# Polysketch attention with a wave MLP: the numerators of two batches as 32 products of 288 columns on 32x32 tiles

## The chip, the cores and the metric

The kernel runs on one core of a Trainium2 chip. The metric is the device time of one execution in microseconds (us); lower is better. The numbers of the trace come from one profiled execution.

## The reference

Sizes: 4 batches (B), 4 heads (H), 1088 positions (S), head width 32 (D), so 128 channels (DM); the sketch has r = 8.

```python
def phi(x):
    a = np.einsum('rd,bhsd->bhsr', S1, x)
    b = np.einsum('rd,bhsd->bhsr', S2, x)
    return np.einsum('bhsi,bhsj->bhsij', a, b).reshape(*x.shape[:-1], r * r)
q_p, k_p = phi(q), phi(k)
kv = np.einsum('bhsf,bhsd->bhfd', k_p, v)
z = np.sum(k_p, axis=2)
num = np.einsum('bhsf,bhfd->bhsd', q_p, kv)
den = np.einsum('bhsf,bhf->bhs', q_p, z)[..., None] + 1e-06
x = (num / den).transpose(0, 2, 1, 3).reshape(B, S, H * D)

theta = x @ w_theta
y = einsum('ts,bsd->btd', w_tok_r, x * cos(theta)) + einsum('ts,bsd->btd', w_tok_i, x * sin(theta))
u = x + y
out = u + np.maximum(u @ w_ch, 0.0)
```

Everything is f32. The denominators can be small, so the sums ahead of the division are held more exactly than one f32 product would; that is why queries, keys and their sketches are split into parts.

## The kernel before, in words

**Layout.** Positions are cut into NC = 9 chunks of 128 (the last one has 64 positions; the buffers are 9 x 128 = 1152 wide), the chunks into NG = 3 groups of GC = 3, so a group has GW = 384 columns. A fully summed f32 product on PE appears in the trace as two records, one for each part of the f32 operands.

**How the work is ordered.** No loop emits instructions directly. Each function calls `op(engine, estimated duration, closure, written, read)` of the class `Layout` (L203; `vop` is the same for DVE), which numbers the operation. Two tables at the top of the file decide the rest: `ORDER` (L34) lists the operations' numbers in the order in which their instructions are issued, which fixes the order on each engine, and `STARTS` (L80) has a planned start for each. `run` (L248) walks through ORDER and gives each buffer, from the planned starts and ends, one slot of its class (`big`: 22 tiles of 1152 words a partition, `zs` 5 of 2176, `hf` 6, `g3` 5 of 768, `g1` 6 of 384, `sm` 13, `ps`: the 8 PSUM banks of 512). `issue` (L267) emits the operations; in a planned gap on PE in the early part it puts idle products (`spin`, L427). Who waits for whom follows from slots and order: a buffer that takes a slot waits for the last reader of the slot's former buffer.

**Stages.** (1) Loads, and the sums over the keys of each batch: `key_sums`, `kfeatures`, `chain`, `chain_out` give for each batch `kvb[b]`, the sums of key features times values. (2) The w_tok matrices are loaded and prepared as `rows[i]`, 17 tiles of 1088 columns. (3) For each batch `query_slices` transposes and scales the queries; `levels` (L1033) multiplies them by the sketch matrices: for each group of three chunks `exact` issues f16 products of parts, and `whole` (L1050) three f32 products whose stationary operand is a chunk of 128 columns of `f` and whose moving operand is `mf[b]` (96 columns). Then DVE combines the parts, forms the denominators and divides one of the two sketches by them.

(4) `outputs_x` (L1088) forms the numerators. For each group of a batch, DVE multiplies the two sketches of the queries to 64 features for each head and position (`outer` into `qp`). In batches 0 and 1 TensorE transposes these and multiplies them by `kvb`. In batches 2 and 3 (`QUADS`) DVE transposes within squares of 32 (L1109, into `qt`, a `g3` buffer), and `quads` (L1112) issues 32 products on 32x32 tiles of the array: two feature halves f, four position squares j, four heads h; the four squares go to four PSUM banks `xq[j]`, the four heads to four strips of 32 partitions, and the second half adds to the first. Each has 96 moving columns (3 chunks x 32 positions). Four copies on ACT (L1121) put the banks into `xt`, x transposed (channels x positions).

(5) For batches 1 to 3 (`XTURN`, L1149) x is brought back to positions x channels on the way through DRAM: DVE transposes in squares of 32 (L1160), SP stores the tile to `far` (L1161) and fetches it with four DMAs (L1165). For batch 3 x is first scaled on ACT (L1155) by a ratio of the largest values of batches 2 and 3, which `balance` (L1229) finds with DVE reductions over both. Beside it run the products with w_theta, sine and cosine on ACT, and then DVE forms `z` = (x cos, x sin) in a `zs` buffer.

(6) The product with w_tok: for batches 0 and 1 `mix_row` (L1256) sums 17 products a column part. Batches 2 and 3 together go through `winograd` (L1352): seven products of halves instead of eight, of sums of quarters of w_tok (DVE and POOL) and differences of z. Products 1 and 2 need z of batch 2 alone; product 5 (L1429) is the first that needs z of batch 3, in a difference with batch 2 (L1427), so the whole round trip of batch 3 lies ahead of it. (7) `finish` (L1282) adds relu(u @ w_ch), transposes and stores; `finish_turned` (L1329) does this for one piece of batch 3 with TensorE transposes, an ACT copy and two products recorded as one operation, into columns of `xT[3]`.

Of the kernel before, what the change touches and what calls it, by code (L numbers as in the profile page):

```python
# [10 lines left out]
F32 = mybir.dt.float32  # L11
# [67 lines left out]
)  # L79
STARTS = (  # L80
# [58 lines left out]
)  # L139
WARM = 0  # L140
FILL = 5.0
LOAD_LEAD = 60.0
RAW_LEAD = 30.0
CHAINS = ((0,), (1,), (2, 3))
# [35 lines left out]
class Layout:  # L180
# [67 lines left out]
    def run(self):  # L248
        slots = {c: [[0.0, None] for _ in range(n)] for c, (n, _) in self.classes.items()}
        for b in self.bufs:  # L250
            b.left = len(b.ops)
# [52 lines left out]
def act(n):  # L304
    return 0.17 + 0.00083 * n
# [1238 lines left out]
```

## Time and profile before

| what | value |
|---|---|
| three runs | 218.03, 218.3, 219.25 us; median 218.3 |
| span of the profiled execution | 215.9 us |
| median of the runs less that span | 2.4 us |
| granted TensorE clock from 78 us on | 1.00 |
| busy: PE, DVE, ACT, POOL | 208.9, 174.3, 114.5, 59.7 us |
| read from and written to HBM | 29.84 and 4.00 MB |

The page of the profile gives the span of the execution's instructions, not a time of the program, so the span is the profiled execution's own time here; the runs of the table above are timed from outside it. Busy times say how full an engine is; which engine sets the end at a given moment is told by the chain of work that ended last, and by the waits. A timeline row has its start in us, its length in us, engine, line, operation, output<-input, tile shape for PE, operand shape and the number of instructions; rows of PE overlap, since a record lasts until its result is written, so the time that a row costs PE is read from its start to the start of the next.

### The profile page before, as it was taken

What the parts mean: (1) busy time and instruction counts of PE and PEld (TensorE: products, weight loads), DVE (VectorE), ACT (ScalarE), POOL (GpSimd) and SP (SyncE); (2) the same over time, 40 slices, a digit from 0 to 9 for tenths busy, and PEclk for the clock granted to TensorE, in tenths of its full rate; (3) what the DMA queues carried; (4) which work ended last, traced back from release to release, by engine and by line L of the source; (5) the groups of instructions that cost most, each with busy time, mean ns of one, the idle gap of its engine ahead of it and who ended that gap; (6) DMA issues with size and microseconds to landing.
All of it is one profiled execution on the core that took longest, in us unless ns stands there. A gap on an engine that the chain in (4) does not pass through costs nothing.

```text
span 215.9 us, 5832 instructions
## 1 busy us (share of the span) xinstructions
PE 208.9 (97%) x2396; PEld 152.8 (71%) x2396; DVE 174.3 (81%) x343; ACT 114.5 (53%) x256; POOL 59.7 (28%) x105
## 2 busy tenths in 40 slices
PE   7899999999999999999999999999999999999992
PEld 7677798868866666866668666667677776666781
DVE  1799998999999998999999798885994747456263
ACT  4899989999998895798704233363810000000000
POOL 1272740306400000604004100000006489950403
PEclk9999999999999999999999999999999999999998
DMA  6999999995998993192002402424050420010735
GB/s 222 395 418 419 384 365 420 425 315 97 360 285 267 416 432 145 75 308 45 0 0 32 74 3 112 114 109 112 2 88 15 67 39 0 0 23 8 125 55 103
DMA packets 28046, 37.09 MB, mean 172 GB/s; under 512 B 20564, under 2 KB 23044, under 8 KB 25844
## 3 DMA queue, kind: packets, MB, share of 16 engines
q1 hardware_dynamic: 22868, 31.86, 42.4%
q0 software_dynamic: 1552, 3.25, 7.2%
q10 hardware_dynamic: 3600, 1.62, 2.8%
q8 instruction: 19, 0.31, 0.6%
q14 instruction: 7, 0.06, 0.1%
HBM read 29.84 MB, written 4.00 MB: 157 GB/s over the span
## 4 chain that ended last, share of the span: by engine, by line
PE 63%; DMA 18%; ACT 14%; issue 2%; SPq 1%; DVE 1%; POOL 1%; POOLq 0%; ACTq 0%
PE ps L399 61%; DMA zs<-w_tok 13%; DMA big<-k_l 5%; ACT big L645 4%; ACT big L643 3%; ACT lv L1056 1%; PE ps L1131 1%; ACT big L1021 1%; ACT g L1199 1%; ACT g L1202 1%; ACT g L1205 1%; ACT g L1203 1%; POOL out L1299 1%; SPq L671 0%; ACT g L1135 0%
## 5 line engine op out<-in xcount | busy, mean ns | idle before, releaser
L399 PE MATMUL ps<-big,zs 128*128 128x384 f32 (+2 forms) x380 | 110.5, 436 | 0.0
L399 PEld LDWEIGHTS ps<-big,zs 128*128 128x128 f32 x380 | 66.9, 190 | 32.5
L379 POOL TENSOR_TENSOR big<-big,big 128x544 f32<-128x544 f32 x16 | 22.1, 1458 | 48.6 <-DVE big L379 44.6
L399 PE MATMUL ps<-big,big 128*32 128x32 f32 (+2 forms) x352 | 22.8, 234 | 0.0
L643 ACT ACTIVATE big<-zs 128x1088 f32<-128x1088 f32 x17 | 20.9, 1231 | 1.5 <-DMA zs<-w_tok 0.9
L379 DVE CUSTOM_DVE_ANT_0 big<-big,big 128x2176 uint16<-128x2176 uint16 x17 | 21.5, 1275 | 0.0
L645 ACT ACTIVATE big<-zs 128x1088 int32<-128x1088 uint32 (+1 forms) x18 | 21.4, 1194 | 0.3 <-DMA zs<-w_tok 0.3
L1338 ACT COPY big<-ps 80x256 f32<-80x256 f32 x1 | 0.4, 368 | 39.6 <-DMA out<-g 39.6
L399 PEld LDWEIGHTS ps<-big,big 128*32 128x32 f32 (+1 forms) x352 | 15.3, 124 | 6.8 <-issue 0.8
L1276 ACT COPY g<-ps 128x384 f32<-128x384 f32 (+1 forms) x6 | 2.5, 466 | 23.4 <-PE ps L399 23.4
L379 DVE TENSOR_TENSOR big<-big 128x544 f32<-128x544 f32 x8 | 9.5, 1204 | 5.6 <-PE ps L399 5.6
L383 DVE TENSOR_SCALAR big<-big 128x1088 int32<-128x1088 int32 x17 | 12.2, 719 | 0.0
L379 POOL TENSOR_TENSOR mf<-mv,sm 128x32 f32<-128x32 f16 (+1 forms) x3 | 0.8, 262 | 39.1 <-DVE sm L379 39.1
L428 PE MATMUL ps<-idle 128*128 128x112 bf16 (+1 forms) x67 | 10.0, 312 | 1.3 <-POOL idle L430 1.3
L379 DVE TENSOR_TENSOR g<-lv 128x768 f32<-128x768 f32 x12 | 11.1, 950 | 0.1
L399 PEld LDWEIGHTS ps<-w,big 128*128 128x128 f32 (+1 forms) x76 | 9.8, 189 | 1.4
L379 DVE TENSOR_TENSOR big<-big,hf 128x1152 f32<-128x1152 f32 x8 | 10.7, 1351 | 0.0
L399 PE MATMUL ps<-w,big 128*128 128x128 f32 (+1 forms) x76 | 10.5, 278 | 0.0
L399 PE MATMUL ps<-sbk,g 128*128 128x64 f32 x72 | 10.0, 276 | 0.3 <-ACT g L793 0.3
L379 DVE TENSOR_TENSOR zs<-zs,g 128x384 f32<-128x384 f32 (+2 forms) x24 | 9.8, 447 | 0.2
L386 DVE SCALAR_TENSOR_TENSOR big<-ps,even,big 128x384 f32<-128x384 f32 (+1 forms) x10 | 4.8, 493 | 6.3 <-PE ps L399 6.2
L1199 ACT ACTIVATE g<-ps 128x384 f32<-128x384 f32 x12 | 5.9, 504 | 7.3 <-PE ps L399 7.3
(199 smaller groups left out, 379.2 us busy)
## 6 DMA issues: line engine op xcount, KB each, us to landing
zs<-w_tok SPq DMA_DIRECT2D x17, 1088.0 KB, 10.6
big<-k_l SPq DMA_DIRECT2D x5, 576.0 KB, 13.2
big<-v_l SPq DMA_DIRECT2D x4, 576.0 KB, 15.6
big<-q_l SPq DMA_DIRECT2D x3, 576.0 KB, 10.7
big<-hf POOLq DMA_DIRECT2D x3, 576.0 KB, 10.0
far<-zs SPq DMA_DIRECT2D x3, 576.0 KB, 2.8
zs<-far SPq DMA_DIRECT2D x12, 144.0 KB, 4.3
big<-k_l ACTq DMA_DIRECT2D x2, 576.0 KB, 4.4
```

What stands on the lines that cost most here:

```text
L379: eng.tensor_tensor(out=o, in0=a, in1=b, op=f)
L383: (eng or V).tensor_scalar(out=o, in0=a, scalar1=s1, scalar2=s2, op0=op0, **kw)
L386: (eng or V).scalar_tensor_tensor(out=o, in0=a, scalar=s, in1=b, op0=op0, op1=op1)
L399: T.matmul(o, lhs, rhs, start=start, stop=stop, skip_group_check=True)
L428: T.matmul(nowhere()[:, :n], idle()[:, 0:P], idle()[:, :n], start=True, stop=True, skip_group_check=True)
L643: op("A", 0.22 + n * 0.0009, lambda: A.activation(dfn(), words_of(raw(), n)[1].bitcast(F32), AF.Prelu, scale=2.0**-112, alpha=-(2.0**32)), ...
L645: op("A", 0.22 + n * 0.0009, lambda: A.activation(stp(), words_of(raw(), n)[0].bitcast(U32), AF.Copy, scale=2.0**-29), [stp], [raw])
L1021: op("A", act(GW) + 0.1, lambda g=g, tr=tr: A.activation(f()[:, g * GW:(g + 1) * GW], tr(), AF.Copy, scale=s()[:, 0:1]), [(f, g)], [tr, (s ...
L1056: op("A", act(480), lambda g=g, lp=lp: A.copy(lv().rearrange("p l (c n) -> p l c n", n=HR)[:, :, g * GC:(g + 1) * GC], lp().rearrange("p c ...
L1131: T.transpose(tr()[:, i * P:(i + 1) * P], qp()[:, i * H + 2 * n:i * H + 2 * n + 2].rearrange("p h i j -> p (h i j)"), ident())
L1199: op("A", act(GW), lambda cs=cs, th=th: A.activation(cs()[:, 0], th(), AF.Copy, bias=ROUND), [(cs, 0)], [th])
L1276: op("A", act(w), lambda: A.copy(u(), yp()[:, :w]), [uT], [yp])
```

## The change

The numerators of batches 2 and 3. The three DVE transposes of a batch write one common buffer `qt` of the class `zs`, and one block per batch issues 32 products of 288 moving columns (9 chunks x 32 positions), where three groups of 32 products of 96 columns stood. Four PSUM banks per batch hold 288 columns each, and four ACT copies of 288 columns replace twelve of 96. The estimate QUAD goes from 0.65 to 1.25. For the common buffer the class `zs` becomes 2304 words wide; `hf` and `sm` have one slot less.

`whole` in `levels` takes for the last chunk only its 64 positions as stationary columns. `finish_turned` has its own buffer `yb` of the class `g1`, and its transposes, copy and products are three operations; an operation without instructions is gone.

The tables. STARTS and the planning in `run` are gone; `SLOTS` names the slot of each buffer and `GAPS` the number of idle products ahead of an operation. The numbers of ORDER after the numerators are other operations than before, since operations were added and removed; the issue order of the early part is kept, and the part from the numerators on is a new order.

```diff
--- before.py
+++ after.py
 ORDER = (
-    29, 32, 4, 2, 5, 0, 1, 3, 34, ...
+    0, 1, 29, 32, 4, 2, 5, 3, 34, ...
...
-STARTS = (
-    73, 73, 90, 92, 103, 130, ...
+GAPS = {11: 3, 57: 3, 79: 3, 110: 1, 203: 8, 153: 1, 77: 5, 86: 2, 163: 1}
+SLOTS = (
+    0, 5, 1, 3, 5, 0, 3, 9, ...
...
-FILL = 5.0
...
-TILE16, TILE32, TILE64, QUAD = 0.045, 0.12, 0.15, 0.65
+TILE16, TILE32, TILE64, QUAD = 0.045, 0.12, 0.15, 1.25
...
     def run(self):
-        slots = {c: [[0.0, None] for _ in range(n)] for c, (n, _) in self.classes.items()}
...
         self.order = [self.ops[i] for i in ORDER]
-        for o, at in zip(self.order, STARTS):
...
-    def issue(self, pools, fill, span):
-
-        last, on = 0.0, False
+        for b, slot in zip([b for b in self.bufs if b.cls is not None], SLOTS):
+            b.slot = slot
+
+    def issue(self, pools, fill):
         for o in self.order:
-            if o.eng == "P":
-                if on:
-                    for _ in range(int((o.start - last - 0.08) * FILL)):
-                        fill()
-                last, on = o.end, on and o is not span[1] or o is span[0]
+            for _ in range(GAPS.get(o.i, 0)):
+                fill()
...
-        "zs": (5, 2176),
+        "zs": (5, 2304),
...
-        "hf": (6, 576),
+        "hf": (5, 576),
...
-        "sm": (13, 192),
+        "sm": (12, 192),
...
             def whole(g=g, o=o):
                 for i in range(GC):
-                    x = f()[:, (g * GC + i) * P:(g * GC + i + 1) * P]
-                    mm(o(i)[:, 2 * HR:], x, mf[b]().rearrange("p t h r -> p (t h r)"), False, i == GC - 1)
+                    c = g * GC + i
+                    n = min(P, S - c * P)
+                    x = f()[:, c * P:c * P + n]
+                    mm(o(i)[:n, 2 * HR:], x, mf[b]().rearrange("p t h r -> p (t h r)"), False, i == GC - 1)
...
         bd = kvb[b]
+        qt = buf("zs", (NC, H, 2, SQ), F32, "qt") if b in QUADS else None
...
             if b in QUADS:
-                qt = buf("g3", (GC, H, 2, SQ), F32, "qt")
-                xq = [buf("ps", (GC, SQ), F32, "xq") for _ in range(NQ)]
-                vop(CH * R * R, lambda qt=qt, qp=qp: V.transpose(out=qt().rearrange("p c h f t -> p (c h f t)"),
-                                                                 in_=qp().rearrange("p n i j -> p (n i j)")), [qt], [qp])
-
-                def quads(qt=qt, xq=xq):
...
-                op("P", QUAD, quads, xq, [bd, qt], hold=[xt])
-                for j in range(NQ):
-                    op("A", act(GC * SQ), lambda g=g, j=j, xq=xq: A.copy(
-                        xt().rearrange("p (c j t) -> p c j t", j=NQ, t=SQ)[:, g * GC:(g + 1) * GC, j], xq[j]()),
-                       cells(xt, g * GW, (g + 1) * GW), [xq[j]])
+                vop(CH * R * R, lambda g=g, qp=qp: V.transpose(
+                    out=qt()[:, g * GC:(g + 1) * GC].rearrange("p c h f t -> p (c h f t)"),
+                    in_=qp().rearrange("p n i j -> p (n i j)")), [(qt, g)], [qp])
                 continue
...
+        if b in QUADS:
+            at("num", b)
+            xq = [buf("ps", (NC, SQ), F32, "xq") for _ in range(NQ)]
+
+            def quads():
+                for f in range(2):
+                    for j in range(NQ):
+                        for h in range(H):
+                            u = slice(j * SQ, (j + 1) * SQ)
+                            mm(xq[j]()[h * D:(h + 1) * D], bd()[u, f, h], qt()[u, :, h, f], f == 0, f == 1)
+
+            op("P", QUAD, quads, xq, [bd, qt], hold=[xt])
+            for j in range(NQ):
+                op("A", act(NC * SQ), lambda j=j: A.copy(
+                    xt().rearrange("p (c j t) -> p c j t", j=NQ, t=SQ)[:, :, j], xq[j]()), [(xt, ("q", j)) if j < NQ - 1 else xt], [xq[j]])
...
     def finish_turned(b, t0, w, u, keys, due):
         po, pu = (buf("ps", (GW,), F32, x) for x in ("po", "pu"))
         n = w // 2
-        y = lambda: xT[b]()[:n, 0:2 * DM]
+        yb = buf("g1", (2 * DM,), F32, "yb")
+        y = lambda: yb()[:n]
+
+        def turned():
+            for c in range(2):
+                T.transpose(pu()[:n, c * DM:(c + 1) * DM], u()[:, c * n:(c + 1) * n], ident())
 
         def products():
-            parts = [u()[:, c * n:(c + 1) * n] for c in range(2)]
-            for c, uc in enumerate(parts):
-                T.transpose(pu()[:n, c * DM:(c + 1) * DM], uc, ident())
-            A.copy(y(), pu()[:n, 0:2 * DM])
-            for c, uc in enumerate(parts):
-                mm(po()[:n, c * DM:(c + 1) * DM], uc, w2()[:, 1], True, True)
-
-        op("P", w * 4 / 2400 + 0.01, products, [po, pu], keys + [w2])
-        vop(w, lambda: stt(y(), po()[:n, 0:2 * DM], 0.0, y(), ALU.max, ALU.add), keys, [po])
-        vop(w, lambda: None, [], keys)
+            for c in range(2):
+                mm(po()[:n, c * DM:(c + 1) * DM], u()[:, c * n:(c + 1) * n], w2()[:, 1], True, True)
+
+        op("P", 0.2, turned, [pu], keys, hold=[yb])
+        op("A", act(2 * DM), lambda: A.copy(y(), pu()[:n, 0:2 * DM]), [yb], [pu])
+        op("P", 0.35, products, [po], keys + [w2])
+        vop(2 * DM, lambda: stt(y(), po()[:n, 0:2 * DM], 0.0, y(), ALU.max, ALU.add), [yb], [po])
```

More of the change, by code (lines that the diff above doesn't have):

```diff
@@ L248, in run @@
     def run(self):
-        slots = {c: [[0.0, None] for _ in range(n)] for c, (n, _) in self.classes.items()}
-        for b in self.bufs:
-            b.left = len(b.ops)
         self.order = [self.ops[i] for i in ORDER]
-        for o, at in zip(self.order, STARTS):
-            o.start = at / 100.0
-            o.end = o.start + o.dur + o.fly
-            for b in o.bufs:
-                if b.slot is None and b.cls is not None:
-                    free = [(s[0], i) for i, s in enumerate(slots[b.cls]) if s[1] is None]
-                    b.slot = min(free)[1]
-                    slots[b.cls][b.slot][1] = b
-            for b in o.bufs:
-                b.left -= 1
-                b.end = max(b.end, o.end)
-                if not b.left and b.slot is not None:
-                    slots[b.cls][b.slot] = [b.end, None]
-    def issue(self, pools, fill, span):
-        last, on = 0.0, False
-        for o in self.order:
-            if o.eng == "P":
-                if on:
-                    for _ in range(int((o.start - last - 0.08) * FILL)):
-                        fill()
-                last, on = o.end, on and o is not span[1] or o is span[0]
+        for b, slot in zip([b for b in self.bufs if b.cls is not None], SLOTS):
+            b.slot = slot
+    def issue(self, pools, fill):
+        for o in self.order:
+            for _ in range(GAPS.get(o.i, 0)):
+                fill()
             for b in o.bufs:
@@ L430 @@
     op("G", 0.3, lambda: G.memset(idle(), 0.0), [idle], [], due=-20.0)
-    first = op("P", 3.2, lambda: [spin(112) for _ in range(39)], [nowhere], [idle], due=-10.0)
+    op("P", 3.2, lambda: [spin(112) for _ in range(39)], [nowhere], [idle], due=-10.0)
     op("V", 1.25, constants, [hm, bdm, halfpi, ones], [])
@@ L1106, in outputs_x @@
             if b in QUADS:
-                qt = buf("g3", (GC, H, 2, SQ), F32, "qt")
-                xq = [buf("ps", (GC, SQ), F32, "xq") for _ in range(NQ)]
-                vop(CH * R * R, lambda qt=qt, qp=qp: V.transpose(out=qt().rearrange("p c h f t -> p (c h f t)"),
-                                                                 in_=qp().rearrange("p n i j -> p (n i j)")), [qt], [qp])
-                def quads(qt=qt, xq=xq):
-                    for f in range(2):
-                        for j in range(NQ):
-                            for h in range(H):
-                                u = slice(j * SQ, (j + 1) * SQ)
-                                mm(xq[j]()[h * D:(h + 1) * D], bd()[u, f, h], qt()[u, :, h, f], f == 0, f == 1)
-                op("P", QUAD, quads, xq, [bd, qt], hold=[xt])
-                for j in range(NQ):
-                    op("A", act(GC * SQ), lambda g=g, j=j, xq=xq: A.copy(
-                        xt().rearrange("p (c j t) -> p c j t", j=NQ, t=SQ)[:, g * GC:(g + 1) * GC, j], xq[j]()),
-                       cells(xt, g * GW, (g + 1) * GW), [xq[j]])
+                vop(CH * R * R, lambda g=g, qp=qp: V.transpose(
+                    out=qt()[:, g * GC:(g + 1) * GC].rearrange("p c h f t -> p (c h f t)"),
+                    in_=qp().rearrange("p n i j -> p (n i j)")), [(qt, g)], [qp])
                 continue
@@ L1331, in finish_turned @@
         n = w // 2
-        y = lambda: xT[b]()[:n, 0:2 * DM]
-        def products():
-            parts = [u()[:, c * n:(c + 1) * n] for c in range(2)]
-            for c, uc in enumerate(parts):
-                T.transpose(pu()[:n, c * DM:(c + 1) * DM], uc, ident())
-            A.copy(y(), pu()[:n, 0:2 * DM])
-            for c, uc in enumerate(parts):
-                mm(po()[:n, c * DM:(c + 1) * DM], uc, w2()[:, 1], True, True)
-        op("P", w * 4 / 2400 + 0.01, products, [po, pu], keys + [w2])
-        vop(w, lambda: stt(y(), po()[:n, 0:2 * DM], 0.0, y(), ALU.max, ALU.add), keys, [po])
-        vop(w, lambda: None, [], keys)
+        yb = buf("g1", (2 * DM,), F32, "yb")
[3 more added lines that the diff above has]
+                T.transpose(pu()[:n, c * DM:(c + 1) * DM], u()[:, c * n:(c + 1) * n], ident())
+        def products():
+            for c in range(2):
[4 more added lines that the diff above has]
+        vop(2 * DM, lambda: stt(y(), po()[:n, 0:2 * DM], 0.0, y(), ALU.max, ALU.add), [yb], [po])
         def store(E, c):
             E.dma_start(out[b, t0 + c * n:t0 + (c + 1) * n, :], y()[:, c * DM:(c + 1) * DM])
-        op("S", w * P * 2 / 100e3, lambda: store(SY, 0), [], keys, due, lk=2)
-        op("A", 0.92, lambda: store(A, 1), [], keys, due, fly=2.1)
+        op("S", w * P * 2 / 100e3, lambda: store(SY, 0), [], [yb], due, lk=2)
+        op("A", 0.92, lambda: store(A, 1), [], [yb], due, fly=2.1)
     def winograd(t):
@@ L1469 @@
         if not bs[0]:
-            last = op("P", 0.1, spin, [nowhere], [kvb[WARM]] if WARM < B else [idle])
+            op("P", 0.1, spin, [nowhere], [kvb[WARM]] if WARM < B else [idle])
     for b in range(B):
@@ L1499 @@
     with tc.manual_schedule():
-        L.issue(pools, spin, (first, last))
+        L.issue(pools, spin)
 def kernel(q, k, v, S1, S2, moe_w_theta, moe_w_tok_r, moe_w_tok_i, moe_w_ch):
```

114 rows, old and new, of tables (ORDER, SLOTS, STARTS) are left out of this document.

## The prediction

> **What bounds the kernel now.** I read the page first: the span, the busy shares, then the chain that ended last.
>
> ```profile
> span 215.9 us, 5832 instructions
> PE 208.9 (97%) x2396; PEld 152.8 (71%) x2396; DVE 174.3 (81%) x343; ACT 114.5 (53%) x256; POOL 59.7 (28%) x105
> PE 63%; DMA 18%; ACT 14%; issue 2%; SPq 1%; DVE 1%; POOL 1%; POOLq 0%; ACTq 0%
> ```
>
> PE is busy for 97% of the span but is only 63% of the chain: busy includes fillers and products with spare time. So the chain itself, in order of time, says where a saving on PE counts.
>
> ```profile
> 66.30 10.64 DMA zs<-w_tok
> ...
> 78.42 3.41 PE ps L399 x55
> ...
> 83.91 25.33 PE ps L399 x133
> ...
> 123.58 86.46 PE ps L399 x601
> 210.06 0.32 DVE big L379
> ...
> 212.39 0.59 POOLq L1540
> ```
>
> Up to 78 us the end is set by loads and ACT; from 78.4 to 210.0 by PE alone, and then come about 6 us of last sums, stores and their landing. The waits of PE from 78 us on confirm it, and busy time by stretches shows who is next.
>
> ```profile
> PE ps L1337 <- DVE big L386: 0.2, 1, 0.2
> ```
> ```profile
> 78.00:109.00 31.00, 30.95 (x237) 21.11 (x226) 29.82 (x54) 23.93 (x43) 5.80 (x12) 1.00 0.41 140
> 109.00:124.00 15.00, 15.00 (x188) 10.75 (x190) 13.48 (x22) 3.54 (x10) 3.04 (x4) 1.00 0.24 38
> 124.00:150.00 26.00, 26.00 (x381) 17.86 (x379) 21.22 (x37) 9.83 (x34) 0.00 (x0) 1.00 0.30 93
> ```
>
> PE waits 0.2 us in all after 78 us, at a granted clock of 1.00. The columns after the length are PE, PEld, DVE, ACT, POOL. So each microsecond that PE no longer needs in this stretch comes off the end one for one, until something else is late; the nearest is DVE, 29.82 busy of 31.00 us up to 109.
>
> **The change part by part.** *The numerators (L1106 to L1124).* They lie wholly in the stretch that PE bounds. Its timeline has six groups of 64 records (32 products, each as two records, the high and the low part of f32) between 119 and 136 us; these rows show two of them, with what stands around:
>
> ```profile
> 126.56 0.96 PE L399 MATMUL ps<-g,g 32*32 32x96 f32 x64
> 127.45 2.74 PE L399 MATMUL ps<-big,zs 128*128 128x384 f32 x8
> ...
> 134.59 0.83 PE L399 MATMUL ps<-w,big 128*128 128x128 f32 x6
> 135.35 0.96 PE L399 MATMUL ps<-g,g 32*32 32x96 f32 x64
> 136.24 0.91 PE L399 MATMUL ps<-big,zs 128*128 128x384 f32 x2
> 136.99 0.81 PE L399 MATMUL ps<-g,w 128*128 128x384 f32 x2
> 137.64 1.45 PE L399 MATMUL ps<-big,zs 128*128 128x384 f32 x4
> 138.93 0.83 PE L399 MATMUL ps<-w,big 128*128 128x128 f32 x6
> 139.59 4.57 PE L399 MATMUL ps<-big,zs 128*128 128x384 f32 x14
> ```
>
> Start to next start, a group takes 0.89 (127.45 less 126.56, 136.24 less 135.35; the other four alike). Its neighbours pay too. Six records of 128 take 0.66 at 138.93 but 0.76 ahead of a group (134.59), so entering costs 0.10. A product of 384 takes 0.645 (two in the 1.29 after 137.64) but 0.75 right behind a group (136.24), so leaving costs 0.10. With both a group is 1.09; six are 6.54.
>
> New are two blocks of 32 products of 288 columns, which no row shows. *From below:* 16 tiles run side by side, with four records each (two products, two parts). A record of 384 columns is half of 0.645, 0.32; one of 288 so about 0.24, and four 0.97. *From above:* three old groups, 2.67, if they overlap no better. (One record after the other is excluded: 64 of 96 columns at 0.08 would be 5.2, and took 0.89.) *Between:* in an old group the four records of a tile are 4 x 0.08 = 0.32, so 0.57 is issue, weight loads and stalls; these go with the number of records, which stays 64. That gives 0.57 + 0.97 = **1.54**, the value I take, as only what streams is scaled. With entering and leaving 1.74; two are 3.48. So 3.48 - 6.54 = **-3.06** (bounds: -4.2 at 0.97, -0.8 at 2.67).
>
> The Trainium skill, "TensorE: Matmul & The Clock Gate", Part 3 (Measured speedup vs the span model), puts a pack of tiles at one product's time plus about 4 ns for each further tile. By it an old group would be four rounds of 0.08 + 0.06, so 0.56; the row says 0.89, so the trace does not agree. By the rule a new block would be an estimated 1.2, and the sum some 0.7 us lower than mine.
>
> *The copies out of PSUM.* 24 copies on ACT become 8 three times as wide.
>
> ```profile
> L1121 ACT COPY big<-ps 128x96 f32<-128x96 f32 x24 | 4.3, 252 | 10.1 <-PE ps L399 10.0
> L793 ACT COPY g<-ps 128x384 f32<-128x384 f32 x12 | 5.4, 476 | 0.0
> ```
>
> Between 0.252 at 96 and 0.476 at 384 lies about 0.40 for 288. ACT is busy 9.83 of 26.00 us there, so nothing is gained or lost by their sum. But they stand at the head of batch 3's chain: the last copy used to end 0.98 after the last group, four of the new, each starting 0.3 after the one before, end about 1.3 after the block. The DVE transposes stay six, of the same size; only their target differs.
>
> *The last chunk of the levels (L1052).* Its stationary operand has 64 columns instead of 128, so these products run in a 128x64 shape.
>
> ```profile
> 89.52 1.48 PE L399 MATMUL ps<-mf,big 128*128 128x96 f32 x12
> ...
> 116.52 1.54 PE L399 MATMUL ps<-mf,big 128*128 128x96 f32 x12
> ```
>
> One chunk per batch; those of batches 2 and 3 are the end of the stretches that begin with these rows, after 78 us. The streamed columns stay 96, so streaming saves nothing. Each adds an entry and an exit, priced above at 0.10 each: **+0.4** for two (bounds 0, if the halved weight load or a neighbouring tile hides them, to 0.6). The other two stand before 78 us, where PE does not set the end: nothing.
>
> The Trainium skill, "TensorEngine Tiling (Array Packing)", Key Properties, says that a change of tiling mode drains TensorE. The 0.10 on either side of a group agrees; nothing in the sum hangs on it.
>
> *The rest.* finish_turned gets a buffer of its own and three recorded steps, with the same instructions. The tables of slots and fillers replace starts: 67 fillers before,
>
> ```profile
> L428 PE MATMUL ps<-idle 128*128 128x112 bf16 (+1 forms) x67 | 10.0, 312 | 1.3 <-POOL idle L430 1.3
> ```
>
> and 67 after. The compiled programs have the same order on every engine through the loads and the first batches (PE for its first 389 rows, DVE 161, ACT 171), so before 78 us I expect no difference. The later part is ordered anew: the same products, sums and DMAs at other places. That costs PE nothing if no wait is added; the waits are rivals below. Behind the last product:
>
> ```profile
> L1299 SPq DMA_DIRECT2D out<-g x13: 315/466/502, 199.2 to 212.3; - x13
> L1299 POOL DMA_DIRECT2D out<-g x8: 597/627/704, 200.0 to 212.4; - x8
> ```
>
> the store queues already work close to the end. If PE finishes 2.7 earlier, the last stores lie closer together; one more store ahead of the last costs 0.47 on SP or 0.63 on POOL: 0 to +0.8, I take **+0.4**.
>
> *Sum:* -3.06 + 0.4 + 0.4 = -2.26. On the profiled execution 215.9 becomes 213.6. The runs' median, 218.3, lies 2.4 above its span; with that unchanged, **216.0**.
>
> **The rivals.** *1. The wide blocks gain little.* They stall between the parts in proportion to width, 2.67 each: -0.8 + 0.4 + 0.4 = 0, so 218.3. For it: what the 0.57 of a group consists of is not shown by a row. Against: the number of records, with which issue and weight loads go, stays. Chance 0.09.
>
> *2. Batch 3's round trip ends last.* The block feeds copies, a balance, a transpose, a store to DRAM and four fetches back, and only then the first product that needs z of batch 3 (named 5, two tiles of class big).
>
> ```profile
> 136.97 0.25 ACT L1121 COPY big<-ps 128x96 f32<-128x96 f32 x1
> ```
> ```profile
> 153.11 1.01 DVE L379 TENSOR_TENSOR zs<-zs,g 128x384 f32<-128x384 f32 x2
> 154.05 0.55 DVE L379 TENSOR_TENSOR big<-zs,zs 128x384 f32<-128x384 f32 x1
> ```
> ```profile
> 145.09 1.73 SPq L1165 DMA_DIRECT2D zs<-far  x4
> 155.70 56.99 SPq L1299 DMA_DIRECT2D out<-g  x29
> ```
> ```profile
> L1165 SPq DMA_DIRECT2D zs<-far x12: 303/430/1001, 93.2 to 146.4; - x12
> ...
> DMA to landing us min/median/max: 2.5/3.9/5.3
> ```
> ```profile
> zs<-far SPq DMA_DIRECT2D x12, 144.0 KB, 4.3
> ```
> ```profile
> 155.68 0.49 PE L399 MATMUL ps<-big,big 128*128 128x384 f32 x1
> ```
>
> Before, the last group is done at 136.24 and its last copy at 137.22; the last fetch is issued at 146.4 and by 4.3 lands at 150.7; two products and a difference on DVE are 1.56, so the operand could be there at 152.3. PE comes to it at 155.68: a margin of 3.4. In the compiled order of the changed kernel the whole block of batch 3 stands where its last group was, but less lies between it and that product: four products of 384 and three of 320 (0.54) fewer, seven of 160 (0.27 by width) more, -2.58 - 1.61 + 1.89 = -2.3. The copies take 0.3 longer. Margin left: 0.8. Besides, eight of the stores that now begin at 155.70 stand on SP directly behind the fetches and share the DMA engines. At 5.3, the slowest landing shown for these transfers, it is 1.0 later, 0.2 past the margin: 216.2. Two microseconds later still, 218.2. To end **slower** than 219.4 it must land 4.2 later than now (0.8 of margin, 3.4 of gain), at 8.5, not far from the 10.64 of the w_tok load in the chain, when the DMA engines were full. PE takes its products in order, so each that follows waits too. Chance 0.12, of it 0.04 for slower.
>
> *3. DVE becomes the bound.* It has no less work while PE has 2.7 less, and was 96% busy up to 109. If the new order leaves it late by 1.5 to 2.5 ahead of a product, the gain there is gone: 217.5 to 218.5; if work that stood in 150 to 170 is now needed earlier too, 219 to 220. Against: from 109 to 150 it has 6.3 us free of 41. Chance 0.12, of it 0.05 for slower.
>
> *4. The change does not do what it says.* The compiled program has 64 products of 288 columns where 192 of 96 stood; excluded.
>
> **How the numbers follow.** Forecast, blocks of 1.2 to 1.9 and no new wait: 216.0 - 0.7 - 0.4 to 216.0 + 0.7 + 0.4, so 214.9 to 217.1, chance 0.67. Rival 1: 218.3, 0.09. Rival 2: 216.2 to 219.5 and beyond, 0.12. Rival 3: 217.5 to 220, 0.12. 0.5% of 218.3 is 1.1, about what a measurement here can tell from no change. Faster, under 217.2: 0.67, with 0.04 of rival 2 and 0.03 of rival 3, 0.74. Slower, over 219.4: 0.02 of rival 1 (blocks above 2.67), 0.04 and 0.05, 0.11. Within: 0.15. Range 214.8 to 218.4: below it lie blocks near 0.97 with no tail cost (0.04), above it the slower cases and a part of rivals 1 and 3 (0.15).
>
> **What the changed profile would show.** Two groups of 64 records with 32x288, each about 1.54 us to the next start (under 1.2 or over 1.9 refutes the sizing); the chain still PE alone from 78.4, ending near 207.3; PE's waits after 78 us below 0.5 in sum, none on DVE ahead of product 5; a last store less than 6.5 us behind PE's end. I am wrong if PE shows a wait on DVE near 154 (rival 2), one between 85 and 135 (rival 3), or if the stretch before 78 us has moved.

## The result, and the profile after

Twenty runs each: median 219.25 us (218.41 to 221.02) with the change, 218.05 (217.4 to 220.84) without. The ratio is 1.0064, 95% interval 1.0043 to 1.0084: **0.6% slower**, where 216.0 was forecast. The profiled execution took 220.3 at a span of 218.5, so a run lies 1.8 above its span. The ratios, here and below, are estimated from the single runs, without those over 1.5% above their kernel's fastest, so they can differ by up to 0.2% from the quotient of two medians.

The page of the changed kernel:

```profile
span 218.5 us, 5303 instructions
PE 210.1 (96%) x2140; PEld 151.5 (69%) x2140; DVE 177.9 (81%) x343; ACT 113.9 (52%) x240; POOL 60.1 (27%) x105
PE 65%; DMA 14%; ACT 8%; DVE 6%; issue 3%; SPq 1%; POOLq 0%; POOL 0%; DVEq 0%; ACTq 0%
```

PE has 256 records fewer and yet 1.2 us more busy time, and DVE, 1% of the chain before, now holds 6% of it. The blocks, by the groups by form and by PE's timeline:

```profile
L332 PE MATMUL ps<-zs,g 32*32 32x288 f32 x128 | 3.2, 412 | 0.0
L1081 ACT COPY big<-ps 128x288 f32<-128x288 f32 x8 | 2.6, 413 | 2.7 <-PE ps L332 2.7
```
```profile
120.87 1.60 PE L332 MATMUL ps<-zs,g 32*32 32x288 f32 x64
122.40 2.10 PE L332 MATMUL ps<-big,zs 128*128 128x384 f32 x6
...
137.30 1.60 PE L332 MATMUL ps<-zs,g 32*32 32x288 f32 x64
138.83 2.10 PE L332 MATMUL ps<-big,zs 128*128 128x384 f32 x6
```

Start to next start a block takes 1.53, both times; 1.54 was the forecast, and a copy takes 0.41 for the forecast 0.40. So the saving is there. PE's waits from 78 us on, and busy time by stretches, show what stands against it:

```profile
PE ps L332 <- DVE big L312: 1.7, 1, 1.7
PE ps L332 <- DVE g L319: 0.2, 1, 0.2
PE ps L332 <- ACT sm L783: 0.2, 1, 0.2
```
```profile
150.00:170.00 20.00, 20.00 (x85) 13.79 (x84) 15.11 (x26) 3.53 (x8) 6.78 (x7) 1.00 0.33 55
170.00:190.00 20.00, 18.06 (x66) 11.47 (x64) 13.34 (x20) 0.00 (x0) 12.73 (x10) 0.91 0.16 27
```

PE waits for DVE, and the granted clock is 0.91 from 170 to 190. PE's timeline at that place:

```profile
174.47 0.81 PE L332 MATMUL ps<-big,zs 128*128 128x384 f32 x2
175.48 0.91 PE L332 MATMUL ps<-big,zs 128*128 128x384 f32 x2 [0.20 <-DVE g L319]
178.13 2.18 PE L332 MATMUL ps<-big,big 128*128 128x384 f32 x4 [1.74 <-DVE big L312]
180.10 1.46 PE L332 MATMUL ps<-g,w 128*128 128x384 f32 x2
181.38 0.45 PE L332 MATMUL ps<-big,big 128*128 128x160 f32 x2
```

From 175.48 to 178.13 PE does one product of 0.645. A row names the shape of its first record; the row at 178.13 holds two records of 384 columns and two of 160, which take 1.97 (178.13 to 180.10) instead of 0.92, and the next two take 1.28 instead of 0.645. So the array runs at about half its rate, and the granted clock of the trace says the same: 0.50 from 177.98 to 181.39, 1.00 on either side. This is called the low clock below. And why DVE was late, from its timeline and POOL's:

```profile
167.91 5.37 DVE L312 TENSOR_TENSOR zs<-zs 128x256 f32<-128x256 f32 x1
173.21 0.55 DVE L312 TENSOR_TENSOR zs<-zs,big 128x384 f32<-128x384 f32 x1
173.67 1.35 DVE L312 TENSOR_TENSOR big<-big 128x544 f32<-128x544 f32 x2
...
176.73 1.34 DVE L312 TENSOR_TENSOR big<-big 128x544 f32<-128x544 f32 x2
```
```profile
168.44 4.55 POOL L312 TENSOR_TENSOR big<-big,big 128x544 f32<-128x544 f32 x3
177.52 1.76 POOL L312 TENSOR_TENSOR big<-big,big 128x544 f32<-128x544 f32 x1 [4.53 <-DVE big L312]
```

A DVE difference of 256 columns, which takes 0.41 elsewhere, stands for 5.37, until POOL's run of three sums is over (168.44 + 4.55 = 172.99). The two sums that PE waits for come at 176.73, as the eighth and ninth operation behind it. The trace of before has the same thing at another place, on DVE and on POOL:

```profile
177.13 4.59 DVE L379 TENSOR_TENSOR big<-big 128x544 f32<-128x544 f32 x1 [2.70 <-PE ps L399]
```
```profile
175.66 5.47 POOL L379 TENSOR_TENSOR big<-big,big 128x544 f32<-128x544 f32 x4
```

There it is 4.59 instead of 0.72, past the end of POOL's run (175.66 + 5.47 = 181.13), but no product near it needed that sum.

What this costs can be summed from PE's records. Take all of them from the first product of 16 columns after 78 us on, each with the interval to the next one's start, and add these up by shape. The numerators fall from 5.35 to 3.06, and the neighbours of the groups take 0.79 less; the last chunks take 0.30 more, the two waits above 2.27 and the low clock 1.69; the 0.54 that is left is spread over single records. The total is 133.75 before and 135.47 after. PE's last rows, of before and after,

```profile
211.57 0.60 PE L399 MATMUL ps<-w,big 128*80 128x128 f32 x4
```
```profile
213.56 0.60 PE L332 MATMUL ps<-w,big 128*80 128x128 f32 x4
```

end at 212.17 and 214.16, so 3.7 and 4.4 us of the span lie behind them.

### The profile page after: what moved, and what is told of

Read it like the earlier page. It is cut to its first block, busy times and chain, and to the rows that moved or that the text cites. A ratio compares the mean times of both kernels' runs of the same rounds, so it can differ in the third digit from the quotient of the medians.

```text
span 218.5 us, 5303 instructions
## 1 busy us (share of the span) xinstructions
PE 210.1 (96%) x2140; PEld 151.5 (69%) x2140; DVE 177.9 (81%) x343; ACT 113.9 (52%) x240; POOL 60.1 (27%) x105
## 4 chain that ended last, share of the span: by engine, by line
PE 65%; DMA 14%; ACT 8%; DVE 6%; issue 3%; SPq 1%; POOLq 0%; POOL 0%; DVEq 0%; ACTq 0%
PE ps L332 60%; DMA zs<-w_tok 11%; DVE big L312 3%; DMA st<-s 2%; PE ps L951 2%; ACT big L578 2%; DMA out<-g 2%; ACT big L626 2%; PE ps L1053 1%; DVE zs L312 1%; ACT g L726 1%; ACT big L576 1%; PE ps L361 1%; DVE g L1240 1%; ACT big L924 1%
## 5 line engine op out<-in xcount | busy, mean ns | idle before, releaser
L332 PE MATMUL ps<-big,zs 128*128 128x384 f32 (+2 forms) x380 | 109.3, 435 | 0.2 <-DVE g L319 0.2
L312 POOL TENSOR_TENSOR big<-big,big 128x544 f32<-128x544 f32 x16 | 22.7, 1528 | 19.6 <-DVE big L312 11.3
L332 PE MATMUL ps<-big,big 128*32 128x32 f32 (+2 forms) x352 | 23.3, 239 | 1.7 <-DVE big L312 1.7
L326 POOL DMA_DIRECT2D g<-big x6 | 5.3, 1049 | 49.3 <-ACT g L1213 49.3
L1139 ACT ACTIVATE g<-g 128x384 f32<-128x384 f32 x12 | 6.3, 530 | 9.1 <-DVE g L319 9.1
L991 ACT COPY lv<-ps 128x480 f32<-128x480 f32 x12 | 6.6, 554 | 8.4 <-PE ps L332 8.1
```

Source lines behind the costliest of these rows:

```text
L312: eng.tensor_tensor(out=o, in0=a, in1=b, op=f)
L326: op("G", 0.9, lambda: G.dma_start(dst(), src(), accum_op=ALU.add), w, r, fly=fly)
L332: T.matmul(o, lhs, rhs, start=start, stop=stop, skip_group_check=True)
L991: op("A", act(480), lambda g=g, lp=lp: A.copy(lv().rearrange("p l (c n) -> p l c n", n=HR)[:, :, g * GC:(g + 1) * GC], lp().rearrange("p c ...
L1139: op("A", act(GW), lambda cs=cs: A.activation(cs()[:, 0], cs()[:, 1], AF.Abs), [(cs, 0)], [(cs, 1)])
```

## The experiments

Each was timed side by side with the kernel before (median 217.93 to 218.31). The last column counts the runs with a mean granted clock of 0.993 or less. Of the kernel before, two of the 96 runs whose clock is on record had one (221.09 and 221.9 us).

| kernel | median | ratio to before, 95% interval | longest wait of PE from 78 us on | low clock |
|---|---|---|---|---|
| changed | 219.25 | 1.0064, 1.0043 to 1.0084 | 1.7 (DVE) | 6 of 20 |
| again | 219.65 | 1.0089, 1.0059 to 1.012 | 1.7 (DVE) | 4 of 12 |
| k1 | 220.03 | 1.0068, 1.0039 to 1.0097 | 2.8 (DVE) | 9 of 12 |
| k2 | 220.21 | 1.0087, 1.0059 to 1.0114 | 2.6 (DVE) | 3 of 6 |
| k3 | 217.71 | 0.9988, 0.9966 to 1.001 | 1.0 (POOL) | 0 of 12 |
| k5 | 218.26 | 0.9987, 0.9965 to 1.0009 | 1.2 (POOL) | 0 of 12 |
| k6 | 220.71 | 1.0092, 1.0064 to 1.0121 | 2.5 (DVE) | 7 of 10 |
| k7 | 217.29 | 0.9956, 0.9935 to 0.9978 | 1.2 (POOL) | 0 of 12 |
| k9 | 217.37 | 0.9954, 0.9934 to 0.9974 | 1.4 (DVE) | 0 of 12 |
| k10 | 215.94 | 0.9914, 0.9883 to 0.9946 | 0.2 (DVE) | 1 of 6 |
| k11 | 215.78 | 0.9919, 0.9888 to 0.995 | 1.5 (ACT) | 2 of 12 |
| k12 | 217.98 | 1.0001, 0.9983 to 1.0019 | 0.5 (DVE) | 0 of 12 |
| k13 | 216.27 | 0.9919, 0.9891 to 0.9948 | 0.5 (DVE) | 0 of 6 |

The table's waits are those that the view of waits gives for the one profiled run. Where the text gives a wait from start to start, less the usual interval, it is some 0.2 longer.

**The changed kernel again.**

> The changed kernel once more, unedited, for a second profile. Theory A: PE waits again about 2 us near 175 for DVE, beside a DVE operation of about 5.4 us that ends with POOL's run of sums; the low clock behind it in about one run of three. If the wait is not there, the loss of the runs at full clock (218.4 to 219.6) has another place, which this trace shows.

The wait (1.7 and 0.2) and the DVE operation (5.37, from 168.04) are there again; this execution has no low clock, and its span is 217.3 against 218.5. So the wait belongs to the program, and the low clock comes in some of its runs only. Its last PE row,

```profile
212.08 0.60 PE L332 MATMUL ps<-w,big 128*80 128x128 f32 x4
```

ends at 212.7, so 4.6 us lie behind PE's end: 0.9 more than before.

**k1: the blocks in the old order.**

```diff
 ORDER (the new operations at the places of those that they replace)
-on PE: ..., 633, 634, 526, 658, 659, 660, 661, 610, 611, 612, 520, 635, 636, 750, 637, 638, ...
+on PE: ..., 612, 659, 750, 633, 526, 634, 635, 762, 769, 613, 660, 614, ...
 SLOTS: given by the old rule
```

750 is the block of batch 3, 762 and 769 are theta products of batch 3, the others products of batches 0 and 1.

> The changed kernel's operations (blocks of 288, narrow last chunks, finish_turned in three steps) in the order of the kernel before: each block and its copies stand where the third group stood, the first theta products of batch 3 wait until the copies are there; slots given anew by the old rule. Theory A, the terms of the sum are right and the new order ate the gain: no wait of PE on DVE near 175, two blocks at 1.53 each, PE's stretch 2.7 shorter than before, time about 215.8 (218.05 - 2.3), ratio 0.989. Theory B, the blocks bring the loss with them (lower clock or waits wherever they stand): 218 to 219, clock below 0.99 in some runs.

Neither theory came out. There is no wait near 175, but there is one ahead of the block of batch 3, with the low clock behind it. PE's rows, then DVE's:

```profile
130.49 1.35 PE L334 MATMUL ps<-big,zs 128*128 128x384 f32 x4
134.66 1.69 PE L334 MATMUL ps<-zs,g 32*32 32x288 f32 x64 [2.82 <-DVE zs L1045]
136.28 1.65 PE L334 MATMUL ps<-big,zs 128*128 128x384 f32 x2
137.72 1.49 PE L334 MATMUL ps<-g,w 128*128 128x384 f32 x2
```
```profile
132.58 0.92 DVE L314 TENSOR_TENSOR g<-lv 128x768 f32<-128x768 f32 x1
133.53 0.98 DVE L1045 STREAM_TRANSPOSE zs<-g 128x768 f32<-128x768 f32 x1
```

DVE ends the third transpose at 134.51, and PE arrives 2.8 earlier. In the kernel before DVE was no sooner done, but PE came later:

```profile
133.49 0.98 DVE L1109 STREAM_TRANSPOSE g<-g 128x768 f32<-128x768 f32 x1 [0.63 <-PE ps L399]
```

There the third group began at 135.35, only 0.9 behind the end of that transpose (134.47). What PE saves ahead of the third group's place it can only use if other work is put there. So the blocks in the old order lose the gain too: the median is 220.03, 1.91 above the 218.12 of before.

**k2: the needed sums first.**

```diff
 ORDER, on DVE
-860, 931, 967, 868, 869, 533, 849, 668, 966, 867, 866, 858
+860, 866, 867, 868, 869, 931, 967, 533, 849, 668, 966, 858
```

866 to 869 are the sums of the tiles 4 to 7, 931 and 967 the differences of z (931 is the one of 5.37), 533 a relu step that reads a PSUM bank.

> The changed kernel, with the two DVE sums that PE waits for near 176 (w_tok tiles 4 and 5 of sums 2) moved ahead of the difference of z that took 5.37 us, and that difference and the next moved behind the sums of tiles 6 and 7. Theory A: whatever DVE does at 168 is still held until POOL is idle near 173, but the needed sums end at about 174.7 instead of 178.07, so the wait of 1.9 and the low clock behind it (1.7) go: 216.0 to 217.3. Theory C, DVE has simply too much work there: the wait stays, or moves to another product by less than 1 us of gain, 218.5 to 219.3.

Theory A was wrong: 220.21. The wait for the sums is gone, and one of 2.6 has taken its place, for 533, which frees its PSUM bank and now stands behind four sums and two differences. PE's waits and DVE's row:

```profile
PE ps L334 <- DVE g L321: 2.6, 1, 2.6
```
```profile
168.62 8.72 DVE L314 TENSOR_TENSOR big<-big 128x544 f32<-128x544 f32 x4
```

Four sums of 0.7 take 8.72 here, the first alone 5.67. So DVE is held here too, though another operation stands first.

**k3: POOL rests while DVE works.**

```diff
 ORDER, on POOL
-642, 619, 890, 889, 891, 893, 935
+642, 619, 893, 890, 889, 891, 935
```

642 and 619 are accumulating DMAs of batch 1; 889 to 891 are sums that wait for nothing late, 893 waits for DVE's 867.

> The changed kernel, with one POOL sum (tile 13 of sums 4, which waits for a DVE sum) moved ahead of three others, so that POOL rests from about 169 until DVE has done the sums that PE needs. Theory A, POOL's back-to-back sums keep the DVE operation of 5.37 us from running: it takes 0.4 to 1.5, DVE's sums end by 175, no wait of PE there, 216.0 to 217.3. Theory C, DVE has too much work and the 5.37 has another reason: it stays above 4 us, and the time at 218.5 to 219.3.

The same DVE operation, with POOL at rest, and the sums that PE needs:

```profile
167.62 0.41 DVE L314 TENSOR_TENSOR zs<-zs 128x256 f32<-128x256 f32 x1
...
172.49 1.35 DVE L314 TENSOR_TENSOR big<-big 128x544 f32<-128x544 f32 x2
```

0.41 instead of 5.37, and the sums 4.2 earlier, with nothing changed but POOL's order. That settles what held it. The time falls by 1.5 to 217.71, not to 217.3 or less, since POOL's sums are now the late ones (waits of 0.25 and 1.17).

The same trace shows that a run of POOL sums does not always shut DVE out for its whole length. Further on POOL does 14 sums in a row, and a DVE operation beside them is held for about one sum:

```profile
173.29 19.39 POOL L314 TENSOR_TENSOR big<-big,big 128x544 f32<-128x544 f32 x14 [4.54 <-DVE big L314]
```
```profile
174.52 0.94 DVE L314 TENSOR_TENSOR zs<-zs 128x384 f32<-128x384 f32 x1
175.38 1.55 DVE L314 TENSOR_TENSOR big<-zs,big 128x256 f32<-128x256 f32 x1
```

In the runs that held DVE throughout, each POOL record starts 0.3 to 0.7 us ahead of the end of the one before it (0.67 at 169.74 in the changed kernel); in this run it is 0.03 to 0.04. What makes the difference was not tested.

**k5: one sum of POOL ahead.**

```diff
 ORDER, on POOL
-642, 619, 893, 890, 889, 891
+642, 619, 890, 893, 889, 891
```

> As k3, but the POOL sum that waits for DVE stands behind the first of the three others instead of ahead of all: POOL does one sum (1.3) in the stretch in which k3 let it rest, and DVE is held 0.8 longer. Theory A: PE's waits on POOL of k3 (0.25 and 1.17) shrink by 1.3, no wait on DVE appears: 217.7 - 1.4 = 216.3. Theory C (DVE has no slack there at all): a wait on DVE of 0.8 comes back and the time stays at 217.5 or above.

Not as expected: the wait for POOL near 187 stays (1.4), and so does the time (218.26). The POOL sum that ends this wait is done at 188.07, in k3 at 187.39.

**k6: k2's order on DVE, POOL in between.**

```diff
 ORDER, on DVE as k2; on POOL
-642, 619, 890, 889, 891, 893
+642, 619, 890, 889, 893, 891
```

> Both moves: DVE's needed sums first as in k2, and on POOL the sum that waits for DVE between the second and the third of the others. POOL then works from 168.4 to 171 and lets DVE go there. Theory A: k2's wait of 2.8 falls to below 0.5, since it came from DVE being held until 173, not from the order of its sums: 216.0 to 217.0. Theory C: wait as in k2, 219 to 220.

Theory A is refuted: 220.71, with a wait of 2.5. DVE's sums begin ahead of POOL's run and are held within it, and again by the next:

```profile
168.18 7.44 DVE L314 TENSOR_TENSOR big<-big 128x544 f32<-128x544 f32 x4
175.54 1.55 DVE L314 TENSOR_TENSOR zs<-zs 128x256 f32<-128x256 f32 x1
```
```profile
168.71 3.27 POOL L314 TENSOR_TENSOR big<-big,big 128x544 f32<-128x544 f32 x2
173.28 3.52 POOL L314 TENSOR_TENSOR big<-big,big 128x544 f32<-128x544 f32 x2 [1.31 <-DVE big L314]
```

Four sums of 0.7 take 7.44. In k2 and k6 another order within DVE did not help against POOL; in k3 it helped that the two did not have such work at the same time.

**k7: the last stores.**

```diff
 ORDER (k5 besides)
-645, 928, ..., 622, ..., 623, ..., 646, ..., 1000, 994
+645, 646, 622, 623, 928, ..., 993, 994, ..., 1000
```

> k5 with the last stores in another order: the transposes and stores of batch 1's last pieces as soon as their sums are there (near 188, where DVE and SP idle) instead of among the last stores, and the POOL store of batch 2's first piece ahead of that of the second. If the tail costs what lies between PE's end and the span's end in k3 (4.4 against 3.7 before), it is 0.6 faster than k5: 215.7. If the last stores' landing sets it whatever is queued ahead: the same as k5 within 0.2.

The median is 217.29, 0.97 below that of k5; the forecast 215.7 counted on a k5 of 216.3. The spans end 4.4 behind PE's last product in k5 and 3.4 in k7; SP issues the same 13 stores from 188 on instead of from 203 (k5, then k7):

```profile
202.81 10.84 SPq L1238 DMA_DIRECT2D out<-g  x13
```
```profile
187.96 24.54 SPq L1238 DMA_DIRECT2D out<-g  x13
```

**k9: the old order, the block later.**

```diff
 ORDER (k1 besides)
-612, 659, 750, 633, 526, 634, 635, 762, 769, 613, 660, 614
+612, 659, 633, 526, 634, 635, 750, 613, 660, 614, 762, 769
 SLOTS: given anew by the old rule (22 of 391 differ from k1)
```

> k1 (blocks in the old order), with four products of batch 1 and of the first batch's output (2.6 us of PE) moved ahead of the block of batch 3, and the theta products of batch 3 behind three others. Theory A: the wait of 2.98 of k1 was DVE not having the third transpose ready before 134.5; with 2.6 us of other work ahead the wait falls to below 0.5 and no low clock follows, while the round trip starts no later: 215.4 to 216.2. Theory B (the loss comes with the blocks): 218 or more, and a low clock in some runs.

The wait ahead of the block falls to 0.2, no run has the low clock, and 217.37 is 2.7 less than k1. It missed 216.2 by a new wait of 1.4, for a PSUM bank that batch 3's theta held longer:

```profile
145.91 2.47 PE L334 MATMUL ps<-big,zs 128*128 128x384 f32 x8 [1.36 <-DVE g L321]
```

**k10: that bank freed.**

```diff
 ORDER (k9 besides): on ACT 763 ahead of 770, on DVE 764 ahead of 709
```

> k9 with one ACT copy and one DVE operation of batch 3's first theta group moved ahead, so that the bank of the first Winograd product is free when PE comes to it. Theory A: k9's wait of 1.52 at 144 goes; PE then reaches product 5 at about 153.8, where its operand is ready at 154.2, so up to 0.5 of wait on DVE comes there: 217.37 - 1.0 to 1.5 = 215.9 to 216.4. If the round trip of batch 3 is then the bound (the second rival of the prediction), the whole 1.5 comes back at product 5: 217.4.

The median is 215.94, and the ratio to before 0.9914 (0.9883 to 0.9946). All waits of PE after 78 us that the view names:

```profile
PE ps L334 <- DVE zs L1045: 0.2, 1, 0.2
PE ps L1276 <- DVE big L321: 0.2, 1, 0.2
```

So the forecast time is reached, in an order in which no product waits long for DVE: 2.07 below the 218.01 of before, of the 2.26 that the sum gave. It is not reached term by term: PE's stretch from the first 16-column product to its last is 1.82 shorter where the sum has 2.66, since some 0.9 of short waits and single intervals is left, and the tail is 3.7 as before where the sum adds 0.4. A DVE sum is still held for 4.58 beside POOL at 175.40, as in the kernel before, and no product near it needs it. Product 5 (at 153.95) finds its operand ready at 152.9.

**k11: the last chunk wide again**, on k10:

```diff
-n = min(P, S - c * P)
+n = P
```

> k10 with the last chunk of the levels as 128 stationary columns again. The narrow chunks cost two entries and exits after 78 us, measured at 0.30 in sum, and the same before it, where PE is not the bound: 0.3 faster than k10 if PE bounds there, the same if DVE does (the block of batch 3 waits for DVE in k9).

The median is 215.78, 0.16 less than k10; the intervals overlap, so the time neither confirms nor refutes the 0.30. The traces do bear it out: from start to start the f32 products of the levels take 4.57 after 78 us in k10, and 4.21 in k11 as in the kernel before. Its profiled run, one of two with a low clock, has it at 80 us, behind a wait of 1.5 for ACT, which itself waited for loads of w_tok, and not in the later part.

**k12: the wait of k1 filled.**

```diff
 def quads():
+    for _ in range(20 if b == 3 else 0):
+        T.matmul(xq[0](), idle[128 x 128], idle[128 x 256], start=True, stop=True)
     for f in range(2):
```

> k1 with 20 idle bf16 products of 256 columns in the wait ahead of the block of batch 3 (2.98, they take about 2.1), into a bank that the block writes anew. If an idle PE brings the low clock behind the wait (318 ns more for each record of 384, 1.65 in sum), the clock stays at 0.995 or above in all runs and the median falls from 220.0 to 218.4. If the blocks themselves bring it, or it comes by chance, the runs stay as in k1: most with a clock of 0.992 or less, median 220.

The median is 217.98 instead of 220.03, and no run of 12 has a low clock instead of 9. The block starts at 134.25 (134.66 in k1), and its neighbours behind it run at full rate:

```profile
131.37 2.35 PE L1076 MATMUL ps<-idle 128*128 128x256 bf16 x20
134.25 1.60 PE L334 MATMUL ps<-zs,g 32*32 32x288 f32 x64 [0.54 <-DVE zs L1045]
135.78 0.91 PE L334 MATMUL ps<-big,zs 128*128 128x384 f32 x2
```

So it is the idle PE that brings the low clock. It costs 1.6 to 1.9: from the start of that block to the end of PE's last product k1's trace takes 1.64 more than k12's, and k1's nine runs with a low clock have a median of 220.09, its three without one 218.19. The Trainium skill, "TensorE: Matmul & The Clock Gate", Part 1, puts the fall to half rate behind an idle window of some 3.4 us. Half rate agrees with the records here, but waits of 1.7 to 2.8 were enough in 10 of 32, 9 of 12, 3 of 6 and 7 of 10 runs (the changed kernel, k1, k2, k6), so a wait needs no such length.

Why only some runs fall is not settled, but the traces say where to look. In all of them the granted clock changes only at whole multiples of 3.41 us from its first record, and a spell at 0.50 within the work lasts 3.41. The 3.41 us just ahead of such a spell held 1.8 us of idle PE in the changed kernel, 2.0 in k1, 2.4 in k6 and 1.5 in k11. In k2's profiled run the wait of 2.6 fell on two such stretches, 1.2 in one and 1.4 in the next, and the clock stayed at 1.00. So it may matter where a wait falls on this grid, which lies differently in each run. A plain threshold does not fit, though: the second profile of the changed kernel had 1.7 in one stretch and no low clock.

**k13: one product more ahead of the block**, on k11:

```diff
 ORDER (k11 besides)
-635, 750, 613
+635, 613, 750
```

> k11 with one more product of batch 1 (0.645) ahead of the block of batch 3. PE waits 0.40 there in k10 and k11; DVE's third transpose is then ready in time: 0.3 to 0.4 faster, 215.4. If the round trip is already the bound, the same as k11.

The median is 216.27: nothing gained. The wait ahead of the block is gone, and two others have come, of 0.5 at 146 for a DVE operation and of 0.2 at 138 for the block's copies on ACT. So by these waits, batch 3's work on DVE and ACT is what PE meets next; product 5 does not wait here either. The third wait of the view, 0.5 for ACT, lies ahead of PE's stretch, at 78 us, as others do in k1, k2 and k6.

## Why the prediction was wrong, point by point

- *"That costs PE nothing if no wait is added":* the step that failed. The sum has no term for waits: it takes the new order's waits as nothing and leaves them to the rivals, without a term for how early each operand is ready. The runs showed waits of 2.27 us in sum, for DVE sums that come late because DVE is held while POOL sums (k3: 5.37 falls to 0.41, and the time by 1.5), and in a third of the runs 1.69 of low clock behind them.
- *Rival 3, DVE becomes the bound (0.12):* the measured 219.25 lies in its 219 to 220, but not by its mechanism. It looked for a DVE short of time, with a wait between 85 and 135 us; the wait came at 176, and DVE is not short of time there (15.11 busy of 20.00 us from 150 to 170 and 13.34 from 170 to 190, the time that it was held counted in). That its number fits is luck.
- *PE alone bounds from 78 to 210 us:* right for the kernel before, and right that a shorter PE shortens the end until something is late. What is late next was named (DVE), but by its share of busy time, not by its margin at the products that need it.
- *Numerators, -3.06:* -2.29 in the groups and -0.79 beside them, -3.08. Right, and the working holds at this second width: what was taken to go with the number of records stays (0.57), what streams grows with the width. The lower figure by the pack rule, 1.2 a block, was too low.
- *Last chunks, +0.4:* +0.30.
- *Stores at the end, +0.4:* +0.6 and +0.9 in the two traces; k7 took 0.97 away by order alone. Mis-sized: I priced one more store in a queue and did not follow the stores through the new order, which starts batch 1's last ones late (SP's last 13 stores begin at 204.87 there and at 199.23 before, with the ends of the spans 2.6 apart).
- *The base, 218.3:* the median of three runs; twenty give 218.05, from which the sum would have said 215.8.
- *Rival 2, batch 3's round trip:* not it. Product 5 did not wait in the changed kernel, in k10 or in k13.
- *Rival 1, the blocks stall:* refuted, 1.53.

The sum with the measured terms, on the median of before: 218.05 - 3.08 + 0.30 + 2.27 + 0.54 + 0.6 to 0.9 is 218.7 to 219.0. The 14 runs without a low clock lie at 218.4 to 219.6, the six others at 220.1 to 221.0. The spread within the 14 was not traced to a cause.

Both causes were to be seen in the trace of before: the DVE sum of 4.59 beside POOL, and the transpose that ended 0.9 ahead of the third group.

The Trainium skill, "SBUF — State Buffer", section "SBUF: two separate sides", says that a VectorE operation with two SBUF inputs and a GpSimd operation that reads SBUF exclude each other by a lock, which the first to start holds for its whole instruction. The runs agree that one stops the other (5.37 against 0.41). They show more: DVE waited through whole runs of two to four POOL sums in the changed kernel, in before, k2 and k6, and for about one sum at a time in k3's long run. Who starts first they do not bear out: by the records the operation of 5.37 starts 0.53 ahead of POOL's first sum (167.91 against 168.44), and it is the one that was held.

## What to carry to other kernels

When work is taken from the engine that bounds, look up for each of its products how long before its turn the operand was ready: these margins, not the other engine's share of busy time, say how much of the saving arrives. A hand-made order is fitted to the durations it was made with; a shorter block at the place of the old one waits (k1), and 2.6 us of other work moved ahead of it and one bank freed brought 2.07 of the 2.26 us (k10). Before sums are put on a second engine in parallel, look for single operations of the first that take many times their mean beside it.

## What the runs showed of the hardware that was not expected

- Waits of PE of 1.7 us or more were followed by a spell of 3.41 us at half rate in many runs (10 of 32 at 1.7, 19 of 28 at 2.5 to 2.8, k1, k2 and k6 together), waits of 1.0 to 1.4 in none of 48 (k3, k5, k7, k9). One of 1.5 was in k11's profiled run. Idle products in the wait prevent it (k12).
- A DVE sum or difference of two SBUF operands took up to 5.67 us beside consecutive POOL sums (k2; 5.37 in the changed kernel), and 0.94 to 1.55 beside others (k3), where 0.38 to 0.72 is usual. DVE operations with a PSUM operand ran beside POOL at their usual length (0.37 and 0.54 where DVE stands beside POOL's sum at 178 in the changed kernel, by its timeline).
- 32 products of 288 columns on 32x32 tiles take 1.53 us for 64 records, three groups of 96 columns 2.67; one copy of 288 columns on ACT takes 0.413 where three of 96 take 0.756.
